# A gated FFT filter and MLP on one core: first MLP product of half the tokens in seven instead of eight block products, tokens outermost; two transform stages on unsplit float32; order made anew

## The chip, the cores and the metric

One core of one Trainium2 chip. The metric is the device time of one execution in microseconds; the runs shown are three executions of the kernel before, and the profile is a further, profiled one.

## The reference

Two branches work on the same x (2048 tokens, 512 features), and a gate per token mixes them. Branch A is a two-dimensional real FFT, a product with learned complex weights, and the inverse FFT. Branch B is an MLP with 1792 hidden units.

```python
def _A_ref(x, w_r, w_i):
    B, S, D = x.shape
    X = (lambda x, axes=(-2,-1): jnp.fft.rfft2(x, axes=axes))(x, axes=(-2, -1))
    W = w_r + 1j * w_i
    X = X * W
    y = (lambda x, s, axes=(-2,-1): jnp.fft.irfft2(x, s=s, axes=axes))(X, (S, D), axes=(-2, -1))
    return y

def _B_ref(x, w1, b1, w2, b2):
    h = jnp.einsum("bsd,df->bsf", x, w1) + b1
    h = _gelu(h)
    return jnp.einsum("bsf,fd->bsd", h, w2) + b2

x = A_x
g = _sigmoid((x * gate_w).sum(-1, keepdims=True))
a = _A_ref(x, A_w_r, A_w_i)
b = _B_ref(x, B_w1, B_b1, B_w2, B_b2)
return g * a + (1 - g) * b
```

## The kernel before

**Split operands.** Everything is float32 outside. For TensorE most operands are split in two tiles of type float32r, a high part h (a copy by ScalarE that rounds) and a low part l (the difference, by VectorE). A product is then three matmuls, h h, h l and l h, added up in PSUM (`prods`, line 506). For most weights the low part is made otherwise (`minus`, line 555): ScalarE writes -h, and an accumulating DMA from GpSimd's queue (`acc`, line 493) adds the weight from HBM.

**MLP** (`mlp`, line 1071). Tokens come in four chunks c of 512; the hidden units in 14 blocks f of 128; features in four blocks q of 128. The first product takes 12 matmuls of 512 columns for each c and f (PSUM tile ph), then gelu in place on ScalarE (line 1127) and the split into g_f h and l (`split`, lines 551 and 552). The second product takes 3 x 7 matmuls for each c and q (PSUM tile po). The hidden blocks go in two halves of seven: all four chunks run with blocks 0 to 6, then all four with 7 to 13. Partial sums go to HBM (bacc). Split x is kept in HBM between the halves (xs, `keep_x`, line 649), and each weight block is loaded and split once (`load_w`, line 1051).

**Transforms.** `forward(j)` (line 686), for 16 groups j of 128 tokens: sums and differences eo and w on VectorE, split of w into eoh and eol (lines 704 and 706), then the feature transform into PSUM tile pd, four matmuls on the high part and four on the low part, whose tables cf hold high and low columns side by side. VectorE splits the result into zb h and l (line 747) and adds the low columns (line 751). Then six matmuls into py, the first token stage. `own_rows` (line 791) mends a few rows with one small product (pown). The later token stages are radix-4 sums on VectorE (`radix4`), and `filt` multiplies by the filter. `inverse(c, h, late)` (line 947) runs eight times with two groups j each: a turn by tables tg (split, lines 956 and 957), its operand pq split into v h and l, eight matmuls into PSUM tile pz, split of pz into zb (lines 990, 991 and 993), and 12 matmuls into pa. Where late is set, its result is added to the output by an accumulating DMA.

**Order.** Each step is entered with its engine, an estimate of its cost, and the buffers that it reads and writes. A planner (`Graph.schedule`, line 311) plays the program through and gives each engine a fixed order. Where several steps are ready, the lowest rank goes first; the ranks are one number a step in the string RANKS. Buffers come in numbered slots per kind, and a step whose buffer has no free slot is passed over. On the chip every engine and queue runs its list in that order. SP issues plain DMAs; GpSimd issues the accumulating ones.

```python
def prods(ps, ah, al, bh, bl, first, last):
    mm(ps, ah, bh, first, False)
    mm(ps, ah, bl, False, False)
    mm(ps, al, bh, False, last)
...
for s, r in zip(g.steps, ranks):
    s.rank = 0.05 * int(r)
order = g.schedule()
```

Of the kernel before, what the change touches and what calls it, by code (L numbers as in the profile page):

```python
# [24 lines left out]
FA = NF // 2  # L25

TE, TW = 320, 576


EXACT = [0, 64, 128, 192]  # L30
NX = len(EXACT)
FORD = np.concatenate([np.arange(1, HD, 2), EXACT, [f for f in range(0, HD, 2) if f not in EXACT], [HD]])
# [23 lines left out]
def _tables():  # L56
# [3 lines left out]
    def cs(c, f):  # L60

        th = 2 * np.pi * np.asarray(f)[None, :] * d / D
        v = -np.sin(th) if c else np.cos(th)
        n = np.array([0.5 if g in (64, 192) else 1.0 for g in f])
        e = np.where(np.abs(v) > 0.6, np.where(n == 0.5, BIG, 1.0), SMALL) * np.sign(v)
        return np.where(np.isin(f, [*EXACT, HD])[None, :], e, v)

    BIG, SMALL = 2276 / 4096, 942.75 / 4096
    factor = np.ones(D)
    factor[128] = np.sqrt(2.0)  # L70
    factor[[64, 192]] = BIG * np.cos(np.pi / 8) + SMALL * np.sin(np.pi / 8)

    cf = np.zeros((2, P, TW), np.float32)
    even = FORD[P + NX:HD]
    for c in range(2):
        h, l = _split(cs(c, FORD[:P]))
        cf[c][:, :P], cf[c][:, P:2 * P] = l, h
        h, l = _split(cs(c, [*EXACT[c:], *even, *([HD] if c else [])]))
        cf[c][:, TE + 2:TE + 2 + P] = h
        cf[c][:, TE + 2 + P:TE + 2 + 2 * P - NX] = l[:, NX - c:P - c]  # L80
        assert not np.delete(l, np.arange(NX - c, P - c), 1).any()
# [8 lines left out]
    ]) / factor[f]  # L90
# [36 lines left out]
    fx = np.stack(_split(fx.reshape(4 * NJ, 4 * NJ)), 1)  # L127
    fx = np.concatenate([fx, fx])
# [306 lines left out]
def tile_kernel(ctx: ExitStack, tc: tile.TileContext, xt, xc, w1, w2, b1, b2, x0g, wf, wrev, out, consts):  # L435
# [41 lines left out]
    def c_pe(n, k=1):  # L477
        return k * (n / 2400 + 0.0135) + 0.005
# [779 lines left out]
    for c in LATE:  # L1258
        stage4(c)
# [63 lines left out]
```

## Time and profile before

| | |
|---|---|
| median of 3 runs | 372.27 us (371.92 to 372.30) |
| span of the profiled execution, first to last instruction | 370.0 us |
| granted TensorE clock, mean | 1.000 |
| DMA moved | 61.20 MB |
| HBM read, written | 41.82 MB, 16.92 MB |

The profile names no other time of its own execution than the span. In rows of groups, `L504` is the helper that records every matmul, so matmuls are told apart by tiles: `ph<-mxh,wa2h` writes PSUM tile ph from operands mxh and wa2h. After the count stand the busy time in us, the mean duration of one in ns, and the idle time of the engine just before it with what ended it. A row of a timeline has the start, the length up to the end of the last one of the row, and how many instructions it merges. In a row of stretches stand from and to, the length, then busy time and count for PE, PEld, DVE, ACT and POOL, the granted clock, the DMA share and GB/s.

### The profile page before, as it was taken

The numbers are of one execution on the slowest core, as the hardware profiler recorded it, in microseconds if no ns is written. First come the engines' busy times: TensorE is split into PE (matmuls) and PEld (weight loads), VectorE is DVE, ScalarE is ACT, GpSimd is POOL, SyncE is SP. The second block draws the span as 40 slices with busy tenths as digits, with TensorE's granted clock in tenths as the row PEclk, the third lists the DMA queues.
The fourth block names the chain that finished last, engine by engine and source line by source line (L and its number), as shares of the span: only waits on it lengthen the run. The fifth ranks groups of instructions, "written<-read, shape, count | busy, mean of one in ns | idle before, by whom it ended". The sixth has DMA issues, their size and how long they took to land.

```text
span 370.0 us, 5589 instructions
## 1 busy us (share of the span) xinstructions
PE 365.0 (99%) x1845; PEld 311.2 (84%) x1845; DVE 337.1 (91%) x748; ACT 224.2 (61%) x415; POOL 34.0 (9%) x54
## 2 busy tenths in 40 slices
PE   8999999999999999999999999999999999999996
PEld 7988888888888888888888888888888888888885
DVE  5999999999999999999989896789688999999993
ACT  5999676678724453555298349753955698653410
POOL 0133000000000000003033010000010000101110
PEclk9999999999999999999999999999999999999999
DMA  8999766195764582586769873216431053276456
GB/s 249 362 267 233 199 201 200 44 271 197 234 222 141 206 288 82 207 217 124 194 161 198 236 167 58 43 37 235 62 51 29 2 204 123 94 177 164 98 155 183
DMA packets 42053, 61.20 MB, mean 165 GB/s; under 512 B 4672, under 2 KB 22528, under 8 KB 41248
## 3 DMA queue, kind: packets, MB, share of 16 engines
q1 hardware_dynamic: 36120, 50.55, 41.5%
q0 software_dynamic: 5472, 9.96, 17.1%
q10 hardware_dynamic: 432, 0.33, 0.3%
q8 instruction: 14, 0.23, 0.2%
q14 instruction: 15, 0.12, 0.2%
HBM read 41.82 MB, written 16.92 MB: 159 GB/s over the span
## 4 chain that ended last, share of the span: by engine, by line
PE 97%; DMA 1%; SPq 1%; ACT 0%; issue 0%; DVE 0%; DVEq 0%
PE ph L504 41%; PE po L504 41%; PE pz L504 4%; PE pd L504 4%; PE py L504 3%; PE pa L504 3%; DMA war<-in_w 1%; PE po_23256r L504 0%; PE po_230r L504 0%; SPq L590 0%; SPq L1060 0%; ACT wa1h L1065 0%; SPq L594 0%; DVE o L1202 0%; PE pown L504 0%
## 5 line engine op out<-in xcount | busy, mean ns | idle before, releaser
L1127 ACT ACTIVATE ph<-ph,b1t 128x512 f32<-128x512 f32 x56 | 36.9, 658 | 51.0 <-PE ph L504 51.0
L963 ACT ACTIVATE sw<-y,al 64x512 f32<-64x512 f32 x32 | 22.9, 721 | 4.6 <-DVE y L826 2.1
L922 DVE TENSOR_TENSOR m<-y,wf 128x514 f32<-128x514 f32 x32 | 20.9, 688 | 0.1
L970 DVE SCALAR_TENSOR_TENSOR pq<-y,al,sw 128x256 f32<-128x256 f32 x32 | 14.6, 480 | 2.9 <-ACT sw L966 2.7
L504 PE MATMUL py<-zb,tf 128*128 128x258 f32 x96 | 16.7, 286 | 0.0
L504 PEld LDWEIGHTS py<-zb,tf 128*128 128x128 f32 x96 | 14.5, 190 | 1.2
L1177 ACT ACTIVATE o<-po,b2t 128x512 f32<-128x512 f32 x8 | 5.4, 688 | 16.6 <-PE po L504 16.5
L778 ACT ACTIVATE y<-pys 64x257 f32<-64x257 f32 x32 | 13.2, 417 | 3.3 <-DVE pys L775 2.6
L495 POOL DMA_DIRECT2D w<-ba x8 | 7.0, 899 | 77.8 <-ACT zb L990 46.2
L504 PEld LDWEIGHTS pa<-zb,ci 128*128 128x128 f32 x96 | 13.1, 190 | 1.0
L504 PE MATMUL pa<-zb,ci 128*128 128x256 f32 x96 | 13.4, 282 | 0.0
L699 DVE TENSOR_TENSOR w<-eo 128x256 f32<-128x256 f32 x32 | 13.0, 418 | 0.1
L696 DVE TENSOR_TENSOR eo<-xf 128x256 f32<-128x256 f32 x32 | 12.9, 416 | 0.0
L704 ACT ACTIVATE eoh<-w 128x512 fp32r<-128x512 f32 (+1 forms) x17 | 10.3, 606 | 4.3 <-DVE w L699 4.3
L495 POOL DMA_DIRECT2D bacc<-o x8 | 7.0, 873 | 63.6 <-ACT o L1181 50.5
L747 DVE TENSOR_TENSOR zb<-pd,zb 128x256 fp32r<-128x256 f32 x32 | 12.5, 417 | 0.3 <-ACT zb L745 0.3
L751 DVE TENSOR_TENSOR zb<-zb,pd 128x256 fp32r<-128x256 f32 (+1 forms) x32 | 12.3, 411 | 0.4
L745 ACT ACTIVATE zb<-pd 128x256 fp32r<-128x256 f32 x32 | 11.1, 384 | 1.6 <-PE pd L504 1.0
L495 POOL DMA_DIRECT2D wa7l<-in_w x1 | 0.9, 872 | 121.3 <-DVE g_1l L552 121.3
L706 DVE TENSOR_TENSOR eol<-w,eoh 128x512 fp32r<-128x512 f32 (+1 forms) x17 | 11.1, 652 | 0.3 <-PE pd L504 0.2
L991 DVE TENSOR_TENSOR zb<-pz,zb 128x512 fp32r<-128x512 f32 x16 | 10.9, 683 | 0.4 <-ACT zb L990 0.3
L990 ACT ACTIVATE zb<-pz 128x512 fp32r<-128x512 f32 x16 | 9.5, 594 | 2.7 <-PE pz L504 2.3
(596 smaller groups left out, 1297.5 us busy)
## 6 DMA issues: line engine op xcount, KB each, us to landing
wf<-in_wf SPq DMA_DIRECT2D x16, 257.0 KB, 3.5
bacc<-o SPq DMA_DIRECT2D x16, 256.0 KB, 2.8
xf<-in_xt SPq DMA_DIRECT2D x14, 256.0 KB, 4.2
wbr<-in_w SPq DMA_DIRECT2D x14, 256.0 KB, 3.6
war<-in_w SPq DMA_DIRECT2D x13, 256.0 KB, 3.9
xm<-in_xc SPq DMA_DIRECT2D x12, 256.0 KB, 4.0
tf<-tf SPq DMA_DIRECT2D x16, 192.0 KB, 3.4
bb<-bacc SPq DMA_DIRECT2D x8, 256.0 KB, 3.7
```

The source lines that it names most:

```text
L495: return add("pool", 2.3 * kb / 340, 3.4, lambda: nc.gpsimd.dma_start(dst(), src(), accum_op=ALU.add), reads, writes, rank)
L504: pe.matmul(ps, w, x, start=start, stop=stop)
L696: v(lambda s=s, op=op: vec.tensor_tensor(eo.ap()[:, s], x.ap()[:, 0:2], x.ap()[:, 2:4], op=op), 256, [x], [(eo, s)], feed)
L699: v(lambda s=s, op=op: vec.tensor_tensor(w.ap()[:, s], eo.ap()[:, :, 0], eo.ap()[:, :, 1], op=op), 256, [eo], [(w, s)], feed)
L706: v(lambda k=k: vec.tensor_tensor(l.ap()[:, k], w.ap()[:, k], h.ap()[:, k], op=ALU.subtract), 256 * len(ps), sub[0] + sub[1], sub[2], feed)
L747: v(lambda c=c: vec.tensor_tensor(segs(xl, c, 0, P + c), segs(ps, c, P, P + 4), segs(xh, c, 0, P + c), op=ALU.subtract), 256, [(ps, c), xh ...
L751: v(lambda o=o, i=i: vec.tensor_tensor(xl.ap()[:, :, o], xl.ap()[:, :, o], ps.ap()[:, :, i], op=ALU.add), 256, [ps], [xl], 0)
L778: a(lambda o=o, i=i: act.activation(Y[j].ap()[o:o + HP, 1], pys.ap()[i:i + HP, 1], AF.Copy), 257, [(pys, 1)], [(Y[j], 1 + k)], 0, more=0.1)
L922: v(lambda mk=mk, k=k, y=y, w=w: vec.tensor_tensor(mk.ap(), y.ap(), w.ap()[:, k:k + 1, :ND].to_broadcast([P, 2, ND]), op=ALU.mult), 514, [ ...
L963: a(lambda sw=sw, y=y, o=o, i=i: act.activation(sw.ap()[o:o + HP], y.ap()[i:i + HP, ::-1, :HD], AF.Copy, scale=al.ap()[i:i + HP, 0:1]), 51 ...
L970: v(lambda sw=sw, pq_=pq_, y=y, j=j, k=k, op=op: vec.scalar_tensor_tensor(pq_.ap()[:, k], y.ap()[:, k, :HD], al.ap()[:, 1 + j:2 + j], sw.a ...
L1127: a(lambda f=f, ps=ps: act.activation(ps.ap(), ps.ap(), AF.Gelu_apprx_tanh, bias=b1t.ap()[:, f:f + 1]), 600, [b1t], [ps], 0.9 if half else ...
```

## The change

Chunks 0 and 1 (CA) keep the first product as it was, but run first, with hidden blocks in three passes (5, 5 and 4). Their x is split from the tiles that the forward transform loads. Chunks 2 and 3 (CB) come behind them, in four passes (4, 2, 4 and 4 blocks). For a unit of two hidden blocks and both chunks, the first product is a product of 2 x 2 blocks with 2 x 2 blocks (two halves of the features inside); it is done with seven block products of six matmuls (`times`). The sums of x blocks (forms 11, t1, t2, 21, t3, 22, t4) are made once, the sums of weight blocks for each unit (`spread_w`). Two PSUM tiles X hold partial results that several outputs share. They are copied by ScalarE into the tiles of other outputs or added by VectorE (`copy`, `plus`), and are taken from the transform's PSUM slots from the first unit on. Since both groups of chunks need the weights, blocks of w2 from the fifth on are written back to HBM once split (ws) and read again; the first four are split again, and w1 is loaded again. Partial sums of a second and later pass are added in HBM by GpSimd's accumulating DMAs (`keep`).

In `forward` and `inverse` the operands of pd and pz stay float32: four matmuls of 129 or 128 columns each, with no split in front and no addition behind. `own_rows` has one float32 matmul. The zb tiles go from four to two of another shape. RANKS is new in full.

```diff
-FA = NF // 2
...
+PASS_A = (range(0, 5), range(5, 10), range(10, 14))
+PASS_B = (range(0, 4), range(4, 6), range(6, 10), range(10, 14))
+CA, CB = (0, 1), (2, 3)
+KEPT = 4
...
-    slots = {"xr": 3, "t2k": 7, "e2": 4, "ttab": 3, "xhl": 4, "w": 29, "hid": 2 * FA,
-             "so": 2, "ba": 2, "bb": 1, "gst": 2, "xm": 2, "pf": 2, "pm": 4, "ti": 1}
-    most = {("pm", "ph"): 2, ("pm", "po"): 2, ("pm", "po0"): 1, ("pm", "py"): 3, ("t2k", "pq"): 2, ("w", "at"): 3, ("w", "bt"): 3}
+    slots = {"xr": 3, "t2k": 7, "e2": 2, "ttab": 3, "xhl": 8, "w": 37, "so": 2, "ba": 2, "pf": 2, "pm": 4, "ti": 1}
+    most = {("pm", "ph"): 2, ("pm", "po"): 2, ("pm", "po0"): 1, ("pm", "py"): 3, ("t2k", "pq"): 2, ("w", "g"): 10, ("w", "gB"): 16,
+            ("w", "ah"): 5, ("w", "al"): 5, ("w", "bh"): 5, ("w", "bl"): 5, ("w", "at"): 2, ("w", "bt"): 2,
+            ("w", "wa"): 13, ("w", "wb"): 8, ("w", "xb"): 4, ("w", "tt"): 2, ("xr", "wr"): 2, ("w", "wt"): 1}
...
+    ws = {(f, k): one(f"sb{f}{k}", [P, D], pool=dp) for f in range(KEPT, NF) for k in "hl"}
...
-        w = buf("t2k", [P, 2, 2, P], F32, f"w{j}", parts=2)
-        h, l = (buf("e2", [P, 2, 2, P], F32R, f"eo{k}{j}", parts=2) for k in "hl")
+        w = buf("e2", [P, 2, 2, P], F32, f"w{j}", parts=2)
...
-        for k in (0, 1) if first else (slice(0, 2),):
-            ps = [k] if first else [0, 1]
-            sub = [[(b, p) for p in ps] for b in (w, h, l)]
-            a(lambda k=k: act.activation(h.ap()[:, k], w.ap()[:, k], AF.Copy), 256 * len(ps), sub[0], sub[1],
-              feed)
-            v(lambda k=k: vec.tensor_tensor(l.ap()[:, k], w.ap()[:, k], h.ap()[:, k], op=ALU.subtract),
-              256 * len(ps), sub[0] + sub[1], sub[2], feed)
...
+        if c in CA:
+            if j < 4:
+                X[c] = new_x(c)
+            split_1(X[c], x, j // 4, c == 0)
...
-        def high(ss=(0, 1), cs=(0, 1)):
-            for s in ss:
-                for c in cs:
-                    o, i = odd if s != c else even
-                    mm(ps.ap()[:, c, o], h.ap()[:, s, c], cft.ap()[:, c, i], s == 0, False)
-        def low():
-            for c in range(2):
-                for s in range(2):
-                    o, i = odd_l if s != c else even_l
-                    mm(ps.ap()[:, c, o], l.ap()[:, s, c], cft.ap()[:, c, i], False, s == 1)
-        if first:
-            for s in range(2):
+        def fold(s, cs):
+            for c in cs:
+                o = slice(HW, 2 * HW) if s == c else slice(0, HW)
+                mm(ps.ap()[:, c, o], w.ap()[:, s, c], cft.ap()[:, c, o], True, True)
+        for s in range(2):
+            if first:
                 for c in range(2):
-                    m(lambda s=s, c=c: high((s,), (c,)), NE, 1, [(h, s), *cf_of(c)], [(ps, c)], 0)
-        else:
-            m(high, NE, 4, [h, cft], [ps], 0)
-        m(low, 236, 4, [l, cft], [ps], 0)
+                    add("pe", c_pe4(HW), 0.25, lambda s=s, c=c: fold(s, (c,)), [(w, s), *cf_of(c)], [(ps, c)], 0)
+            else:
+                add("pe", c_pe4(HW, 2), 0.25, lambda s=s: fold(s, (0, 1)), [(w, s), cft], [ps], 0)
...
-        for o, i in ((slice(0, P), slice(0, P)), (slice(P + NX, 2 * P), slice(3 * P + NX, 4 * P))):
-            v(lambda o=o, i=i: vec.tensor_tensor(xl.ap()[:, :, o], xl.ap()[:, :, o], ps.ap()[:, :, i], op=ALU.add), 256, [ps],
-              [xl], 0)
...
-            vh, vl = split(f"v{j}", "e2", [P, 2, HD], pq_, lambda y: y, 512)
-            ps = buf("pf", [P, 2, 2, 2 * P], F32, f"pz{j}", pool=pq)
-            def some(x, k, high, t=t, ps=ps):
+            ps = buf("pf", [P, 2, 2, P], F32, f"pz{j}", pool=pq)
+            def turn(k, t=t, ps=ps, pq_=pq_):
                 for ft in range(2):
-                    mm(ps.ap()[:, ft, k] if high else ps.ap()[:, ft, k, :P], x.ap()[:, k, ft * P:(ft + 1) * P],
-                       t.ap().rearrange("p a b -> p (a b)") if high else t.ap()[:, 0], high, not high)
-            def rest(some=some, vh=vh, vl=vl):
-                some(vl, 0, False)
-                some(vh, 1, True)
-                some(vl, 1, False)
-            m(lambda some=some, vh=vh: some(vh, 0, True), 256, 2, [t, vh], [ps], FEED)
-            m(rest, 248, 6, [t, vh, vl], [ps], FEED)
-            a(lambda n=n, ps=ps: act.activation(zh.ap()[:, :, :, n], ps.ap()[:, :, :, :P], AF.Copy), 512, [ps], [(zh, n)])
-            v(lambda n=n, ps=ps: vec.tensor_tensor(zl.ap()[:, :, :, n], ps.ap()[:, :, :, :P], zh.ap()[:, :, :, n], op=ALU.subtract),
+                    mm(ps.ap()[:, ft, k], pq_.ap()[:, k, ft * P:(ft + 1) * P], t.ap(), True, True)
+            for k in range(2):
...
+                add("pe", c_pe4(P, 2), 0.25, lambda k=k, turn=turn: turn(k), [t, (pq_, k)], [ps], FEED)
...
-            v(lambda n=n, ps=ps: vec.tensor_tensor(zl.ap()[:, :, :, n], zl.ap()[:, :, :, n], ps.ap()[:, :, :, P:], op=ALU.add),
-              512, [ps], [(zl, n)], FEED)
...
+        if n == "b" and f >= KEPT:
+            for k, b in zip("hl", (h, l)):
+                dma(lambda k=k, b=b: sp.dma_start(ws[f, k].ap(), b.ap().bitcast(F32)), 256, [b], [ws[f, k]])
...
+    def keep(c, q, o, ps, first, sign):
+        where = [(bacc[c], 2 * q), (bacc[c], 2 * q + 1)]
+        def dst():
+            return bacc[c].ap()[:, q].rearrange("p a b -> p (a b)")
+        if first:
+            b = nb2 if sign < 0 else b2t
+            a(lambda: act.activation(o.ap(), ps.ap(), AF.Identity, bias=b.ap()[:, q:q + 1], scale=sign), 600, [b, ps], [o])
+            dma(lambda: sp.dma_start(dst(), o.ap()), 256, [o], where)
+        else:
+            a(lambda: act.activation(o.ap(), ps.ap(), AF.Copy, scale=sign), 512, [ps], [o])
+            acc(dst, lambda: o.ap(), 256, [o], where)
...
+    def early_x():
+        new_forms(("11", "t1", "t2"))
+        for e in range(2):
+            b00, b01, b11 = (raw_x(k, n, e, "xr", "xe") for k, n in ((0, 0), (0, 1), (1, 1)))
+            put("11", e, b00)
+            less(b01, b01, b00)
+            put("t1", e, b01)
+            less(b11, b11, b01)
+            put("t2", e, b11)
+            dma(lambda e=e, b11=b11: sp.dma_start(t2s[e].ap(), b11.ap()), 256, [b11], [t2s[e]])
+    def spread_x():
+        new_forms(("21", "t3", "22", "t4"))
+        for e in range(2):
+            b10, b11, b01 = (raw_x(k, n, e, "w", "xb", [free[CA[0]]]) for k, n in ((1, 0), (1, 1), (0, 1)))
+            t = buf("w", [P, 4 * P], F32, f"tt{e}", cls="tt")
+            dma(lambda t=t, e=e: sp.dma_start(t.ap(), t2s[e].ap()), 256, [free[CA[0]], t2s[e]], [t])
+            put("21", e, b10)
+            less(b01, b11, b01)
+            put("t3", e, b01)
+            put("22", e, b11)
+            less(t, b10, t)
+            put("t4", e, t)
...
+    def spread_w(u, late):
+        f0, f1 = 2 * u, 2 * u + 1
+        H = slice(0, HD), slice(HD, D)
+        r = [buf("xr", [P, D], F32, f"wr{f}", cls="wr") for f in (f0, f1)]
+        for x, f in zip(r, (f0, f1)):
+            dma(lambda x=x, f=f: sp.dma_start(x.ap(), w1[f]), 256, [] if u else t2s, [x])
+        ta = buf("t2k", [P, D], F32, f"ws{u}", cls="ws", parts=2)
+        T = {}
...
+        h, l, b = tile_("0h"), tile_("0l"), tile_("1", 2)
+        a(lambda: act.activation(h.ap(), r[0].ap(), AF.Copy), 512, [r[0], *late], [h])
+        minus(h, l, lambda b: b.ap(), 512, lambda: w1[f0], ([h], [l]), 1)
+        a(lambda: act.activation(b.ap()[:, H[0]], r[1].ap()[:, H[1]], AF.Copy), 256, [r[1], *late], [(b, 0)])
+        v(lambda: vec.tensor_tensor(b.ap()[:, H[1]], r[1].ap()[:, H[1]], b.ap()[:, H[0]], op=ALU.subtract), 256, [r[1], (b, 0)], [(b, 1)])
+        sub(ta, 0, r[1], 0, r[1], 1, ALU.add)
+        sub(ta, 1, ta, 0, r[0], 0)
+        sums("s", ta)
+        sub(r[1], 0, r[0], 0, r[1], 0)
+        sub(r[1], 1, r[0], 1, ta, 1)
+        sums("t", r[1])
...
+            def times(o, i, j, start, A=A):
+                bs, w = A[i]
+                def emit():
+                    k = 0
+                    for e in range(2):
+                        for wi, xi in ((0, 0), (0, 1), (1, 0)):
+                            first = start and k == 0
+                            pe.matmul(o.ap(), w(wi, e), FX[j].ap()[:, xi, e], start=first, stop=k == 5, skip_group_check=not start)
+                            k += 1
+                m(emit, 512, 6, [*bs, FX[j]], [o])
...
+            def done(ps, i, n, u=u):
+                f, c = 2 * u + i, CB[n]
+                gelu(ps, f)
+                if end:
+                    v(lambda: vec.scalar_tensor_tensor(ps.ap(), gb.ap()[:, c], 1.0, ps.ap(), op0=ALU.subtract, op1=ALU.mult),
+                      512, [gb], [ps])
+                G[n, f] = split(f"g{c}_{f}", "w", [P, 512], ps, lambda x: x, 512, cls="gB")
+            times(N[0], "11", "11", True)
+            times(N[1], "s1", "t1", True)
+            copy(X[0], N[0])
+            five = buf("t2k", [P, 512], F32, f"five{u}", cls="five")
+            copy(five, N[1])
+            times(X[0], "s2", "t2", False)
+            times(N[0], "12", "21", False)
+            done(N[0], 0, 0)
+            copy(X[1], X[0])
+            times(X[0], "s3", "t3", False)
+            times(X[1], "s4", "22", False)
+            plus(X[1], X[1], five)
+            done(X[1], 0, 1)
+            plus(N[1], X[0], five)
+            done(N[1], 1, 1)
+            times(X[0], "22", "t4", False)
+            done(X[0], 1, 0)
...
+    early_x()
+    for p in range(len(PASS_A)):
+        for c in CA:
+            mlp(p, c)
     for q0 in range(4):
         filt(q0)
-    for n, c in enumerate(ORDER[:2]):
+    for c in CB:
         stage4(c)
-        inverse(c, 0, False)
-        inverse(c, 1, False)
-    for c in LATE:
+        for h in range(2):
+            inverse(c, h, False)
+    for c in CA[::-1]:
         stage4(c)
-    for c in SECOND:
-        mlp(1, c)
-        if c in LATE:
-            inverse(c, 0, True)
-            inverse(c, 1, True)
+    spread_x()
+    for p in range(len(PASS_B)):
+        fast(p)
+        if p < 2:
+            for h in range(2):
+                inverse(CA[1 - p], h, True)
     ranks = RANKS.split()
     assert len(ranks) == len(g.steps)
```

More of the change, by code (lines that the diff above doesn't have):

```diff
@@ L1152, in mlp @@
[L1152 to L1165 removed]
+            o = buf("so", [P, 4 * P], F32, f"o{p}_{c}{q}", parts=3)
@@ L1196, in last @@
             s = slice(h * 2 * P, (h + 1) * 2 * P)
             y = Y[c + 8 * h + 4 * (q // 2)]
-            if n.start and not b:
+            if end and h:
                 for k, e in enumerate((sp, act)):
```

377 lines of the change are left out of this document (164 added, 213 removed), and 154 rows, old and new, of the table RANKS.

## The prediction

> **What bounds the kernel now.** I read first the page's head, its busy line and its chain of waits, then the busy time by stretch, then the order of time on TensorE.
>
> ```profile
> span 370.0 us, 5589 instructions
> PE 365.0 (99%) x1845; PEld 311.2 (84%) x1845; DVE 337.1 (91%) x748; ACT 224.2 (61%) x415; POOL 34.0 (9%) x54
> PE 97%; DMA 1%; SPq 1%; ACT 0%; issue 0%; DVE 0%; DVEq 0%
> 0.00:12.50 12.50, 10.93 (x67) 10.14 (x67) 8.37 (x27) 7.51 (x15) 0.65 (x16) 1.00 0.88 280
> 12.50:60.80 48.30, 48.30 (x274) 42.25 (x273) 46.33 (x124) 40.43 (x89) 7.19 (x8) 1.00 0.86 240
> 60.80:190.00 129.20, 129.20 (x618) 108.63 (x617) 125.11 (x275) 72.69 (x137) 5.83 (x8) 1.00 0.61 186
> 340.00:370.00 30.00, 26.57 (x143) 22.80 (x141) 22.75 (x49) 6.49 (x11) 3.47 (x4) 1.00 0.57 158
> ```
>
> TensorE has work without a gap from 12.5 us nearly to the end, at full granted clock (1.00 in every stretch). Only 5.0 us are idle, at the start and behind the last matmul. So time is the number of matmuls times their spacing, as long as the other engines keep up. VectorE is the one that might not: it is busy 46.33 of 48.30 and 125.11 of 129.20 us in the middle stretches.
>
> The duration of a matmul holds its drain, so I take spacings, from start to start.
>
> ```profile
> 99.67 0.39 PE L504 MATMUL po<-g_5h,wb5h 128*128 128x512 f32 x1
> ...
> 102.84 0.39 PE L504 MATMUL po<-g_6h,wb6l 128*128 128x512 f32 x1
> 5.49 1.04 PE L504 MATMUL ph<-mxh,wa0h 128*128 128x128 f32 x8
> 6.37 0.33 PE L504 MATMUL ph<-mxl,wa0h 128*128 128x256 f32 x1
> 59.78 0.64 PE L504 MATMUL pd<-cf,eoh 128*128 128x254 f32 x4
> 60.27 0.56 PE L504 MATMUL pd<-cf,eol 128*128 128x130 f32 x4
> 60.67 0.33 PE L504 MATMUL py<-zb,tf 128*128 128x258 f32 x1
> 227.79 0.40 PE L504 MATMUL pz<-tg,v1h 128*128 128x256 f32 x2
> 228.03 0.40 PE L504 MATMUL po<-g_10h,wb10h 128*128 128x512 f32 x1
> 229.41 0.33 PE L504 MATMUL pz<-tg,v1l 128*128 128x128 f32 x2
> 229.58 0.45 PE L504 MATMUL pz<-tg,v1h 128*128 128x256 f32 x2
> 229.87 0.34 PE L504 MATMUL pz<-tg,v1l 128*128 128x128 f32 x2
> 230.04 0.44 PE L504 MATMUL ph<-mxh,wa9h 128*128 128x512 f32 x1
> ```
>
> The first and last of 15 rows give 3.17 / 14 = 0.2264 us for 512 columns; 256 columns take (228.03 - 227.79) / 2 = 0.12. The slope is 0.106 us over 256 columns, 0.416 ns a column, with 0.0136 us fixed. A matmul of 128 columns would be 0.067 by that line, yet eight with a new weight each take (6.37 - 5.49) / 8 = 0.110: there the weight load sets the spacing. The first transform costs 60.67 - 59.78 = 0.89 us per row group j (eight matmuls), the turning stage pz 0.24 + 0.17 + 0.29 + 0.17 = 0.87.
>
> **The change, first on TensorE.** (a) For chunks 2 and 3, seven pairs of hidden blocks need 7 products of 6 matmuls instead of 8: 336 become 294. That is -42 x 0.2264 = -9.5 us. Chunks 0 and 1 and the whole second product keep their counts.
>
> (b) Both unsplit stages become four float32 matmuls of 129 or 128 columns, 128 in all. No float32 matmul stands in this trace. Lowest end: one such matmul costs as much as the 128-column row, 0.110, and the stages come to 16 x (0.44 - 0.89) + 16 x (0.44 - 0.87) = -14.1. Highest end: four partial products, each with its own weight load, 0.44, so 16 x (1.76 - 0.89) + 16 x (1.76 - 0.87) = +28.2. Between them: two operands of two halves make four partial products, which stream 4 x 129 columns, 4 x 129 x 0.416 ns + 0.0136 = 0.228; and two weight loads (a high and a low half, each used twice) make 2 x 0.110 = 0.220. Two reckonings meet, so I take 0.228: 16 x (0.91 - 0.89) + 16 x (0.91 - 0.87) = +1.0 us.
>
> The Trainium skill (FP8 and Floating Point Precision, TensorE Precision Notes) counts four passes for true float32, which at this slope is the 0.228 taken. But the Trainium skill (TensorE: Matmul & The Clock Gate, Weight-path perf modes) says that the fast load is off for float32, with an estimate of columns / 1.2 = 107 ns a load; if each pass had its own, that is 0.43 and +27 us. No float32 load stands in this trace; the row of 0.110 has the plain rate already, which speaks for equal loads.
>
> (c) Small ones: two zero matmuls, +0.45; the own-rows product one float32 matmul of 257 columns (4 x 257 x 0.416 ns + 0.0136 = 0.44) for two of 0.12, +0.2; the last column block split whole, under +0.1. Sum of (a) to (c): -7.8 us.
>
> (d) Handovers. A group's first matmul can come late:
>
> ```profile
> 31.07 0.50 PE L504 MATMUL ph<-mxh,wa6h 128*128 128x512 f32 x1
> 31.40 0.39 PE L504 MATMUL ph<-mxl,wa6h 128*128 128x512 f32 x1
> ```
>
> 0.33 here instead of 0.2264. Seven groups a unit instead of four in the same place are 49 for 28, at up to 0.1 each +2.1; none for those that come in a row. I take +1.0.
>
> Sum: 370.0 - 7.8 + 1.0 = 363.2 us of span. The page gives no time of the profiled execution but this span; the median of the runs is 372.27, 2.3 above it, which I keep: **365.5 us**.
>
> **What must stay beside it.** Prices of the other engines:
>
> ```profile
> L706 DVE TENSOR_TENSOR eol<-w,eoh 128x512 fp32r<-128x512 f32 (+1 forms) x17 | 11.1, 652 | 0.3 <-PE pd L504 0.2
> L751 DVE TENSOR_TENSOR zb<-zb,pd 128x256 fp32r<-128x256 f32 (+1 forms) x32 | 12.3, 411 | 0.4
> L993 DVE TENSOR_TENSOR zb<-zb,pz 128x512 fp32r<-128x512 f32 x16 | 10.9, 682 | 0.2
> L957 DVE TENSOR_TENSOR tg<-ti,tg 128x128 fp32r<-128x128 f32 x16 | 4.6, 285 | 2.0 <-ACT tg L956 2.0
> L552 DVE TENSOR_TENSOR g_2l<-ph,g_2h 128x512 fp32r<-128x512 f32 x4 | 2.7, 684 | 0.2 <-ACT g_2h L551 0.2
> L699 DVE TENSOR_TENSOR w<-eo 128x256 f32<-128x256 f32 x32 | 13.0, 418 | 0.1
> L1127 ACT ACTIVATE ph<-ph,b1t 128x512 f32<-128x512 f32 x56 | 36.9, 658 | 51.0 <-PE ph L504 51.0
> L704 ACT ACTIVATE eoh<-w 128x512 fp32r<-128x512 f32 (+1 forms) x17 | 10.3, 606 | 4.3 <-DVE w L699 4.3
> L956 ACT ACTIVATE tg<-ti 128x128 fp32r<-128x128 f32 x16 | 4.9, 309 | 4.9 <-DVE ti L954 4.7
> L1181 ACT ACTIVATE o<-po 128x512 f32<-128x512 f32 x8 | 4.7, 593 | 7.2 <-PE po L504 7.0
> L495 POOL DMA_DIRECT2D bacc<-o x8 | 7.0, 873 | 63.6 <-ACT o L1181 50.5
> bacc<-o POOLq DMA_DIRECT2D x8, 256.0 KB, 4.1
> xs0l<-mxl SPq DMA_DIRECT2D x4, 256.0 KB, 2.9
> mxh<-xs0h SPq DMA_DIRECT2D x1, 1024.0 KB
> q1 hardware_dynamic: 36120, 50.55, 41.5%
> q0 software_dynamic: 5472, 9.96, 17.1%
> ```
>
> VectorE loses L706, L751, L993, L957 and the 16 low halves of v (0.684 each, 10.9): 49.8 us. It gains 14 of 512 elements for x (eight differences, and 22 low halves instead of 16: 9.6), per unit five of 256 and two of 512 for the weight sums (7 x 3.46 = 24.2) and two additions (14 x 0.684 = 9.6): 43.4. So 337.1 - 6.4 = 331, and 331 / 363 is 91% as before. ScalarE loses 10.3, 4.9 and 16 high halves of v (9.7); it gains some 45 copies at 0.606 (four and a half a unit for the weights, eight for the four w2 blocks split again, six for x; 27.3) and at 0.593 the 21 copies within PSUM products and 24 more evictions (26.7): 224 + 29 = 253 us, 70%. Its order is hidden under TensorE unless a copy stands on the seven-product chain, below.
>
> GpSimd's accumulating DMAs go from 38 to 73 (32 partial sums for 8; 14 + 8 + 4 + 7 weight low halves for 22; 8 outputs as before): 34 + 35 x 0.873 = 65 us of issue, and queue 0 to 33% of the DMA engines. SP's queue drops the x copies (24 of 256 KB out, six of 1024 KB in, 12.6 MB) and adds the w2 copies (20 of 256 KB out and 20 in, 10.5) and 18 reloads of w1 and w2 (4.7), with x some 55 MB for 50.55: 45%. Together 78% instead of 59: room on average. An eviction buffer is held 0.593 + 0.873 + 4.1 = 5.6 us; there are two, so one per 2.8 us. The pass of two hidden blocks fills one per 6 x 0.2264 = 1.36 us, eight in 20.4 us with its unit's products, where 22.4 are needed: 2 us late at most, and the next unit can be done in that time, so 0 to +2 for the range.
>
> **Rivals.** *The seven-product chain stalls TensorE* (slower). All units share one PSUM pair X. Behind a unit's last product X is freed by a gelu (0.658), a copy (0.593) and a low half (0.684), then refilled by a copy (0.593): 2.53 us, against the next unit's two free-standing products, 12 x 0.2264 = 2.72. With empty queues it just holds; if each of these four waits behind one other operation (three on ScalarE, one on VectorE, 2.5 us more), each unit is 2.3 us late. Second products of the pass before can fill it (a pass of four blocks has 96 matmuls, 21.7 us). Where the order places them elsewhere, half the delay stays: 7 x 1.2 = +8, 373.5 us. It decides from 0.97 us a unit (6.8 / 7). For it: ScalarE's work grows most. Against: today TensorE is without a gap from 12.5 to 190 us.
>
> *Float32 loads its weights for each partial product*: 0.44 a matmul, 27 us more, 393 us; three loads, 0.33, 379. This is what the Trainium skill's rule on the fast load would do here if it met every pass. The gain is gone from 0.281 (0.228 + 6.8 / 128). Against it, only that the two reckonings meet.
>
> *VectorE becomes the bound.* 331 us at today's 91% is the span forecast, so nothing is to spare. Splits, which TensorE's first passes wait for, now fall in the half that also has all forward transforms. If 1% of its work is uncounted or idle in the wrong place, 3.6 us: 369.
>
> **How the numbers follow.** Forecast 0.64, with a range of its own from 362.5 to 368.5 (handovers 0 to 2.1, evictions 0 to 2, one more us either way for float32 between 0.220 and 0.236); chain stalls 0.14 at 369 to 379; float32 loads 0.10 at 378 to 393; VectorE 0.12 at 367 to 373. The range for 8 in 10 is 361 to 378: it leaves out most of the float32 case, the worst chain stalls and a float32 cheaper than 0.22. About 0.2%, 0.75 us, is what a measurement of this kernel can tell. Faster: 0.64, a fifth of the chain case (0.03), and over half of VectorE's (0.07), 0.74; within 0.2%, 0.05; slower, 0.21.
>
> **What would show it.** Right: TensorE busy near 357 us and still about 98%; spacing of four float32 matmuls in pd and pz near 0.91; VectorE near 331. Wrong in the float32 step: that spacing at 1.3 or 1.8. Wrong in the chain step: TensorE idle or stretched inside each unit, ended by ScalarE's copy into X or VectorE's low half. Wrong in VectorE's: gaps on TensorE before 200 us, ended by VectorE. If TensorE's busy time falls by 8 and the span does not, the gain went into waits.

## The result and the profile after

The changed kernel takes 384.67 us (median of 4 runs, 383.3 to 387.13) against 372.28 beside it: ratio 1.0342 [1.0304, 1.038]. Measured again with the experiments it took 383.18 us, ratio 1.0277 [1.0246, 1.0308]. The forecast was 365.5, faster; it is slower by 11 to 12 us.

The page of the changed kernel, its span, its busy times and its chain of waits:

```profile
span 383.6 us, 5725 instructions
PE 365.0 (95%) x1808; PEld 301.5 (79%) x1808; DVE 328.8 (86%) x729; ACT 250.9 (65%) x459; POOL 64.5 (17%) x83
...
PE 58%; DMA 11%; issue 10%; ACT 8%; DVE 8%; POOL 2%; SPq 1%; POOLq 0%; DVEq 0%; ACTq 0%
```

The work is what was forecast: VectorE 328.8 us (331 forecast), ScalarE 250.9 (253), GpSimd 64.5 (65). What changed is the chain: TensorE holds 58% of it, not 97%; DMA, ScalarE and VectorE hold 27%. TensorE's busy time is 365.0 as before although 40 matmuls of 512 columns are gone on balance (42 less two of zeros). A matmul is recorded as busy for 0.39 us, while the next one starts after 0.2264 where nothing holds it up, so a wait shorter than the difference hides in busy time. Starts of matmuls tell more. The last row of TensorE in each kernel's order of time, changed kernel first, then the kernel before:

```profile
377.92 0.28 PE L493 MATMUL poB<-g_13h,wb13lb 128*128 128x256 f32 x1
```

```profile
366.29 0.28 PE L504 MATMUL po_23256r<-g_13h,wb13l 128*128 128x256 f32 x1
```

The last matmul starts 11.63 us later with 40 x 0.2264 = 9.1 us less to do: TensorE lost 20.7 us more on its way there than before. Behind it the span has 5.7 us instead of 3.7. 20.7 - 9.1 + 2.0 = 13.6, the difference of the spans.

What TensorE waited for in the changed kernel (us in all, times, longest):

```profile
PE ph L493 <- DVE g_10l L542: 2.3, 1, 2.3
PE ph L493 <- DVE g_8l L542: 1.6, 1, 1.6
PE ux L1159 <- DVE ux L1174: 1.4, 1, 1.4
...
PE ux L1159 <- ACT ux L969: 0.9, 1, 0.9
PE ph1u L1159 <- DVE g_1l L542: 0.8, 1, 0.8
PE ux L1159 <- ACT g_0h L541: 0.8, 1, 0.8
PE ph1u L1159 <- DVE g_3l L542: 0.7, 1, 0.7
```

The two longest stand in the first MLP half, beside the filter; those on `ux` (the pair X) and `ph1u` (a unit's other tile, `N[1]` in the code) stand in the units of seven products. VectorE in turn waited for transfers:

```profile
DVE wf L831 <- DMA wf<-in_wf: 7.5, 5, 3.1
DVE b0d L738 <- DMA y<-ownr: 5.4, 1, 5.4
```

Busy time by stretch (TensorE, its loads, VectorE, ScalarE, GpSimd, then granted clock, DMA share, GB/s), the kernel before and then the changed one:

```profile
100.00:160.00 60.00, 60.00 (x267) 49.64 (x266) 58.37 (x116) 26.23 (x42) 0.87 (x1) 1.00 0.58 193
...
200.00:260.00 60.00, 60.00 (x293) 50.68 (x292) 51.91 (x111) 34.08 (x60) 6.12 (x8) 1.00 0.53 133
```

```profile
100.00:160.00 60.00, 56.06 (x234) 44.37 (x233) 48.65 (x102) 28.09 (x47) 14.02 (x16) 0.97 0.88 203
160.00:200.00 40.00, 40.00 (x178) 33.09 (x178) 38.54 (x78) 23.46 (x43) 10.55 (x12) 1.00 0.88 212
200.00:260.00 60.00, 56.54 (x254) 44.67 (x253) 48.22 (x103) 47.40 (x83) 7.04 (x8) 1.00 0.52 127
```

Two places, then. From 100 to 160 us the DMA engines are busy 0.88 of the time instead of 0.58, VectorE has 9.7 us less work done, TensorE 33 matmuls less. From 200 to 260 us the transfers are as before (0.52), VectorE has room, and TensorE still does 39 matmuls less. A third, smaller loss is the wait of 1.4 us on `ux`, at 346 us. A high DMA share alone costs nothing: from 160 to 200 us it is 0.88 too, and TensorE is busy throughout.

A unit of seven products, in the order of time of the changed kernel (start, duration, engine, and in brackets the idle time before it and its releaser). `ux` is both halves of X:

```profile
205.65 0.70 DVE L1168 TENSOR_TENSOR ph1u<-ux,five 128x512 f32<-128x512 f32 x1
...
206.38 0.66 ACT L969 ACTIVATE ux<-ux,b1t 128x512 f32<-128x512 f32 x1 [1.35 <-DVE ph1u L1168]
...
207.08 0.60 ACT L541 ACTIVATE g_0h<-ux 128x512 fp32r<-128x512 f32 x1
...
207.73 1.66 PE L1159 MATMUL ux<-xft,wa 128*128 128x512 f32 x6 [0.81 <-ACT g_0h L541]
...
209.49 0.69 DVE L542 TENSOR_TENSOR g_0l<-ux,g_0h 128x512 fp32r<-128x512 f32 x1 [1.74 <-PE ux L1159]
...
210.22 0.66 ACT L969 ACTIVATE ux<-ux,b1t 128x512 f32<-128x512 f32 x1 [0.50 <-DVE g_0l L542]
...
211.58 0.74 PE L1159 MATMUL ph1u<-xft,wash 128*128 128x512 f32 x2 [0.82 <-DVE g_1l L542]
```

Read against the code: the GELU at 206.38 is of X's second half, which was ready at 205.62; it waited for VectorE's `N[1] = X[0] + five`, which reads the first half. The product at 207.73 goes into the first half; it waited for the high part of the second half's GELU. The low half at 209.49 reads the second half; it waited for that product. No data passes in any of the three. The waits are in the program itself (each line is an instruction, with what it waits for; +512 is the second half):

```
PE   ux+0   <- x, wa          waits for ScalarE: g_0h <- ux+512
DVE  g_0l   <- ux+512, g_0h   waits for TensorE: ux+0 <- x, wa (the product's last matmul)
ACT  ux+0   <- ux+0, b1       waits for VectorE: g_0l <- ux+512
ACT  ux+512 <- ux+512, b1     waits for VectorE: ph1u <- ux+0, five
```

X is one tensor of two halves of 512 columns, and in these four places the program orders accesses to both halves as one. The hand-made order takes them as separate.

### The profile page after: what moved, and what is told of

Read it like the earlier page. It is cut to its first block, busy times and chain, and to the rows that moved or that the text cites. A ratio compares the mean times of both kernels' runs of the same rounds, so it can differ in the third digit from the quotient of the medians.

```text
span 383.6 us, 5725 instructions
## 1 busy us (share of the span) xinstructions
PE 365.0 (95%) x1808; PEld 301.5 (79%) x1808; DVE 328.8 (86%) x729; ACT 250.9 (65%) x459; POOL 64.5 (17%) x83
## 3 DMA queue, kind: packets, MB, share of 16 engines
q1 hardware_dynamic: 37472, 53.65, 44.2%
q0 software_dynamic: 10512, 19.14, 31.6%
## 4 chain that ended last, share of the span: by engine, by line
PE 58%; DMA 11%; issue 10%; ACT 8%; DVE 8%; POOL 2%; SPq 1%; POOLq 0%; DVEq 0%; ACTq 0%
PE po L493 17%; PE ph L493 14%; PE poB L493 9%; PE ux L1159 6%; PE pd L493 3%; PE py L493 3%; DMA wbr<-in_w 3%; PE ph0u L1159 2%; DMA wb1l<-in_w 2%; PE pz L493 2%; PE ph1u L1159 2%; POOL bacc L484 2%; DMA bacc<-oB 2%; ACT sw L875 2%; DMA y<-ownr 1%
## 5 line engine op out<-in xcount | busy, mean ns | idle before, releaser
L969 ACT ACTIVATE ph<-ph,b1t 128x512 f32<-128x512 f32 x28 | 18.4, 659 | 34.3 <-PE ph L493 32.7
L484 POOL DMA_DIRECT2D bacc<-oB x16 | 13.9, 869 | 70.4 <-ACT oB L1047 56.3
L484 POOL DMA_DIRECT2D bacc<-o x16 | 14.8, 943 | 50.0 <-ACT o L1047 45.9
L493 PEld LDWEIGHTS pz<-tg,pq 128*128 128x128 f32 x128 | 16.4, 191 | 4.5 <-issue 1.2
L1047 ACT ACTIVATE o<-po 128x512 f32<-128x512 f32 x16 | 9.4, 596 | 15.6 <-DMA bacc<-o 11.0
L493 PE MATMUL pz<-tg,pq 128*128 128x128 f32 x128 | 17.5, 278 | 1.4 <-ACT sw L878 0.7
L493 PE MATMUL pd<-cf,w 128*128 128x129 f32 x128 | 17.4, 275 | 0.0
L1159 PE MATMUL ph0u<-xf,wa0h 128*128 128x512 f32 x56 | 17.4, 392 | 0.0
L493 PEld LDWEIGHTS pd<-cf,w 128*128 128x128 f32 x128 | 16.3, 191 | 0.9 <-DVE logit L683 0.3
L1159 PE MATMUL ux<-xft,wa 128*128 128x512 f32 x42 | 11.4, 407 | 3.2 <-DVE ux L1174 1.4
```

The source lines that it names most:

```text
L484: return add("pool", 2.3 * kb / 340, 3.4, lambda: nc.gpsimd.dma_start(dst(), src(), accum_op=ALU.add), reads, writes, rank)
L493: pe.matmul(ps, w, x, start=start, stop=stop)
L969: a(lambda: act.activation(ps.ap(), ps.ap(), AF.Gelu_apprx_tanh, bias=b1t.ap()[:, f:f + 1]), 600, [b1t], [ps]).table = "gelu"
L1047: a(lambda: act.activation(o.ap(), ps.ap(), AF.Copy, scale=sign), 512, [ps], [o])
L1159: pe.matmul(o.ap(), w(wi, e), FX[j].ap()[:, xi, e], start=first, stop=k == 5, skip_group_check=not start)
```

## The experiments

The theories: **A**, the halves of X wait for each other though no data passes. **B**, the chain of sums is too long by itself. **C**, the transfers of the new arrangement come late to VectorE, which works in order. **D**, the unsplit float32 stages are a gain of their own.

**Two tensors for X.** A place of two halves becomes two tensors, everywhere it is used:

```diff
-            self.t = self.pool.tile(self.shape, self.dt, tag=f"{self.tag}_{self.slot}", ...)
+            self.t[k] = self.pool.tile([P, 512], F32, tag=f"{self.tag}_{self.slot}_{k}", ...)
...
-        X = [View(free["X"], k, 1, lambda t, k=k: t[:, k]) for k in range(2)]
+            X[k].ap = lambda k=k: free["X"].bank(k)
```

> The changed kernel with its output and order, but the two halves of the pair X are two tensors of one bank each instead of two halves of one tensor (and the other tiles of that place likewise, with the gate's column sum in two instructions and one addition). In the profile after, TensorE's last product of the first unit into the first half starts at 207.7 us, when ScalarE's upper half of the other half's GELU ends, although it needs nothing of it; four such waits of 0.9 to 1.0 us stand between 207 and 226 us, two of 0.3 by 240 and one of 1.6 at 346. Theory A (the program makes the halves wait for each other): TensorE's waits of 207 to 240 us shrink from 4.4 to under 1 us and the time falls by 4 to 6 us, to 378.5 to 380.5. Theory B (the chain of sums itself is too long for its cover, true dependences only): the same waits stay, ended by VectorE's additions and lows, and the time stays within 1 us of 384.7. Theory C (the loss is in the new order's transfers, in the first half): within 1 us of 384.7 too, and the waits of 107 to 160 us stay under A, B and C alike.

375.37 us, ratio to before 1.0103 [1.0058, 1.0149]: 9.3 us below the first measurement of the change, 7.8 below the second. The edit reaches more than X: the tiles pd, pz and pa have the same place and are parted too. The same moment in its order of time, and the stretch:

```profile
203.50 0.60 ACT L548 ACTIVATE g_0h<-uxk 128x512 fp32r<-128x512 f32 x1
...
204.12 1.52 PE L1172 MATMUL uxk<-xft,wa 128*128 128x512 f32 x6
204.69 0.68 DVE L549 TENSOR_TENSOR g_0l<-uxk,g_0h 128x512 fp32r<-128x512 f32 x1
...
206.92 0.73 PE L1172 MATMUL ph1u<-xft,wash 128*128 128x512 f32 x2
```

```profile
200.00:260.00 60.00, 59.87 (x283) 49.26 (x283) 53.27 (x113) 51.26 (x91) 7.03 (x8) 1.00 0.58 144
```

The product no longer waits, the low half runs beside it, and no wait on X or `ph1u` is left in TensorE's list. TensorE does 283 matmuls in the stretch instead of 254. Counted from the first matmul of the first unit to the last matmul of the kernel, this run is 7.4 us shorter than the first profile of the change and 7.6 shorter than the second. Of these, 4.1 stood in front of matmuls into X and 1.9 in front of those into `ph1u`, the rest mostly in front of pa and pz. So theory A holds, with 6.0 us where it promised 4 to 6; what is left of the 9.3 came from the other parted tiles and from before the units, where the transfers differ from run to run. All sums are still there, so B alone does not hold. The wait of 1.7 us for `g_8l` at 112 us stays, as A, B and C all had it.

**No sums.** The two copies into X, the copy `five` and the two additions of each unit are not issued; the place of every other step is kept.

```diff
-                a(lambda: act.activation(o.ap(), i.ap(), AF.Copy), 512, [i], [o])
+                a(lambda: None, 512, [i], [o])
...
-                v(lambda: vec.tensor_tensor(o.ap(), i.ap(), s.ap(), op=ALU.add), 512, [i, s], [o])
+                v(lambda: None, 512, [i, s], [o])
```

> The changed kernel with the same order, without the five copies and additions of each unit of seven products (partial sums are left out; every product, GELU, split and transfer stays). Theory A (halves wait for each other): the waits between the halves' GELUs, splits and products stay for the most part, so TensorE loses 3 us or more between 200 and 240 us, and the time falls by 1 to 3 us, to 381.5 to 383.5. Theory B (the chain of sums is what stalls TensorE): all of the second half's waits go, 6 us or more, to 378 or less. Theory C (transfers of the first half): within 1.5 us of 384.7.

375.94 us, 1.0134 [1.0084, 1.0185]: the number is B's, not A's 381.5 to 383.5. TensorE's waits on `ux` are gone, but those on the unit's other result remain:

```profile
PE ph1u L1159 <- DVE g_1l L542: 0.8, 1, 0.8
PE ph1u L1159 <- DVE g_3l L542: 0.7, 1, 0.7
```

Taken with the run above: the sums together with the false waits make the chain, and removing either breaks it. With the halves apart the sums fit their cover; that is why the first edit keeps all work and gains as much. The false waits do stay without the sums, as I had thought, but off TensorE's path: in this run's order of time, at 205.27 us, the low half still waits 1.12 us for the product, and at 206.00 the GELU 0.58 for that low half. The product itself no longer comes late, since no addition holds up the GELU in front of it.

**Neither stores nor write-back.** The 20 stores of the split second weight and the two transfers of own rows are not issued; the later loads of that weight read another table of the same size.

```diff
-                dma(lambda k=k, b=b: sp.dma_start(ws[f, k].ap(), b.ap().bitcast(F32)), 256, [b], [ws[f, k]])
+                dma(lambda: None, 256, [b], [ws[f, k]])
...
-            add("sp", 0.2, 2.6, lambda k=k: sp.dma_start(yy.ap()[k * HP:k * HP + 1], ...), [r], Y)
+            add("sp", 0.2, 2.6, lambda k=k: None, [r], Y)
```

> The changed kernel with the same order, without the 20 stores of the split second weight (its later loads read another table of the same size) and without the two transfers that write the corrected own rows back. In the profile after, SyncE's queue sends the filter's rows behind a store that waits for its split, VectorE waits for them, and TensorE stands 2.4 us at 154.9 and then runs nine matmuls at half clock; at 111.5 it stands 1.8 us for a VectorE that waited 5.4 us for the own rows. Theory C (transfers queued in order): these two waits and the slow stretch go, and the time falls by 5 to 7 us, to 378 to 380. Theories A and B: the early time is caught up or lost again later, and the time falls by less than 2 us, to 383 or more.

377.35 us, 1.0141 [1.0126, 1.0156]; C's range was 378 to 380. VectorE's wait for own rows is gone, that for the filter's rows falls from 7.5 us to:

```profile
DVE wf L831 <- DMA wf<-in_wf: 0.8, 2, 0.6
```

TensorE's waits for `g_8l` and `g_10l` are no longer listed, those on X all stay (1.4, 0.9, 0.8, 0.8, 0.7). So C is a second cause, in another place.

**The changed kernel once more, and both edits together.** The run without sums, whose edit touches only the second half, already differed from the change at 155 us, so the change itself was profiled again. (The expectation counts the two-tensor run as untouched up to 195 us as well; but its edit also parts pd, in the first half.)

> The changed kernel itself, unaltered, once more, beside the kernel below: how much of the profile's waits is the same in another execution. If the wait of 2.4 us at 154.9 us belongs to the program, it is there again and the time is 383 to 387. If it is an accident of the transfers (the filter's rows landed 6.9 us after their issue in that profile, 5.1 and 5.8 us in the two runs with other edits that touch nothing before 195 us), it is absent in this profile and the time is 379 to 383.

383.18 us: just inside the first branch by its time, and the second by its profile. The wait at 154 us is down to 0.3 us in TensorE's list, but that at 111 us is longer, and slow matmuls follow it (last section):

```profile
PE ph L493 <- DVE g_8l L542: 1.8, 1, 1.8
```

The waits on X are the same in both profiles to a tenth of a us (0.9, 0.8, 0.8, 1.4). What varies from run to run is which transfer comes late; that one does is in both.

> The changed kernel with the two edits at once: X as two tensors, and neither the stores of the split second weight nor the write-back of the own rows. Each alone came to 375.4 and 377.4. If the two causes stand apart (halves that wait for each other in the second half, transfers in the first), their gains add up but for the wait at 155 us, which both lost: 384.7 - 9.3 - 7.3 + 3 = 371, range 369 to 373. If the second only makes up for the first, the time stays at 375.

370.8 us, 0.9958 [0.9937, 0.9979], as the sum of the two causes had it (371). They stand apart, in the main.

**Each half of that edit alone.**

> The changed kernel with the same order, without the two transfers that write the corrected own rows back into the filter's rows (the stores of the second weight stay). The two edits of the run before last took 7 us together against the first measurement and 6 against the second. If the own rows' way back is the larger part, TensorE's wait at 111 us (1.8 and 2.0 us, the longer one with seven matmuls at half clock behind it) is gone and the time is 379 to 381; if the stores are, that wait is gone too but the time is 381.5 to 383.

> The changed kernel with the same order, without the 20 stores of the split second weight alone (the later loads read another table of the same size). If the stores' traffic is what makes the filter's rows and the corrected rows late, the wait at 154 us is gone, that at 111 us shrinks by half or more, and the time is 378 to 380. If they only fill the wires where nobody waits, the wait at 111 us stays at 1.7 to 2.0 us and the time is 381.5 to 383.

Without the write-back 383.51 us (1.0305 [1.0288, 1.0322]): nothing gained, less than either branch had. The wait at 111 us is gone, and the next one, at 153 us, stands in its place (1.8 us; 2.3 and 0.3 in the two profiles of the change). TensorE's and VectorE's waits of that run:

```profile
PE ph L493 <- DVE g_10l L542: 1.8, 1, 1.8
...
DVE wf L831 <- DMA wf<-in_wf: 7.5, 5, 2.6
```

Without the stores 378.53 us (1.0175 [1.0148, 1.0201]), in the range of the first branch. VectorE's waits:

```profile
DVE b0d L738 <- DMA y<-ownr: 5.1, 1, 5.1
DVE wf L831 <- DMA wf<-in_wf: 3.6, 3, 2.2
```

It still waits 5.1 us for the own rows, but TensorE's wait for `g_8l` is no longer listed; that for `g_10l` is 1.1, where I had it gone. The stores' traffic is the larger part: 4.7 to 6.1 us. Without the own rows' way back as well it was 377.35, 1.2 us less; the intervals of the two runs overlap, so it is not shown that this way back costs anything by itself.

**Another order of the same steps.** X as two tensors, every engine's steps in a sequence of my own making.

> The changed kernel with X as two tensors and another order of the same steps: moved on each engine so that VectorE's lows and the half-weights stand ahead of work that waits for transfers, laid out with the own rows' way back at 4.7 us as the profile shows it and not 2.8. Nothing is left out. If order alone was what remained of the loss, the waits at 112, 284 and 291 us of the two-tensor run shrink and the time is 371 to 374; if the transfers simply take that long for any order of this work, it stays at 375 or more.

377.45 us, 1.0138 [1.0123, 1.0153], 2 us more than the two tensors in the order as given, though the intervals overlap. The waits moved rather than went:

```profile
PE ph L512 <- DVE y L724: 1.7, 1, 1.7
PE po L512 <- DMA wb0l<-in_w: 1.6, 1, 1.6
PE po L512 <- ACT o L1067: 1.5, 1, 1.5
```

This shows that this order is no better, not that none is.

**Float32 stages alone.** The kernel before, with the stages on unsplit float32 (the matmul below for the split ones, no splits of `w`, `v` and `tg`, own rows as in the change). In the first try the priorities were kept and the planner arranged the steps anew; in the second each engine's old sequence was held. The second also has four `zb` tiles and four slots for the float32 operands (`e2`); the first, like the change, has two of each.

```diff
-                    mm(ps.ap()[:, c, o], h.ap()[:, s, c], cft.ap()[:, c, i], s == 0, False)
...
-                    mm(ps.ap()[:, c, o], l.ap()[:, s, c], cft.ap()[:, c, i], False, s == 1)
+                mm(ps.ap()[:, c, o], w.ap()[:, s, c], cft.ap()[:, c, o], True, True)
```

> The kernel before, in its own order and with its own eight products, with only the two transform stages and the own rows on unsplit float32. Theory D (float32 is no loss: 0.80 and 0.83 us for four of its matmuls in the profile after, against 0.89 and 0.87 for the split form): TensorE has 2.2 us less and VectorE some 40 us less, and the time is 369.5 to 371.5, faster than both kernels. Rival (unsplit stages cost TensorE their handovers, one weight load more exposed at each float32 matmul): 373 or more.

> The kernel before with its eight products and, unlike the first try of this, every engine's steps held in the sequence that they had before (a step that is gone is left out of the line, a float32 matmul takes the place of the split one), with only the two transform stages and the own rows on unsplit float32. Nothing is left out. The first try came to 375.3 with TensorE's own work 2.5 us less but its waits 6.4 us more, in the first 100 us. Theory D (float32 is a gain, and the first try's loss was its rearranged order): the waits go back to 4 to 5 us and the time is 369 to 370.5, below both kernels. Rival (the shorter stage no longer covers its handovers, whatever the order): the waits at py's products stay and the time is 372 or more.

The first: 375.29 us, 1.008 [1.006, 1.01], slower than the kernel before by 3. Its waits:

```profile
PE py L485 <- ACT pys L728: 1.0, 1, 1.0
PE py L485 <- issue: 0.8, 1, 0.8
```

The second: 371.8 us, 0.9995 [0.9981, 1.0009], no difference that can be told; its waits are gone, and its busy line reads:

```profile
PE 365.0 (99%) x1845; PEld 309.8 (84%) x1845; DVE 294.3 (80%) x648; ACT 202.8 (55%) x365; POOL 33.9 (9%) x48
```

VectorE has 42.8 us less than before and ScalarE 21.4, TensorE exactly as much, and so is the time. Theory D falls: I had read the gain off the spacing of the float32 rows alone. Here is why, in the changed kernel's order of time (a float32 matmul leaves two records):

```profile
61.95 1.05 PE L493 MATMUL pd<-cf,w 128*128 128x129 f32 x8
62.76 0.97 PE L493 MATMUL py<-zb,tf 128*128 128x258 f32 x6
63.56 0.39 PE L493 MATMUL ph<-mxh,wa4h 128*128 128x512 f32 x1
```

Four float32 matmuls take 0.81 us to the next start, but the six behind them take 0.80 where 6 x 0.12 = 0.72 is due. Together 0.89, what the eight split ones took before. (The split ones left a delay too: the `py` behind them, at 60.67 us of the profile before, took 0.16 to the next start for 0.12. By these rows float32 would be 0.04 us a group cheaper, 1.3 us in 32 groups; the interval of the second try leaves room for 0.7.) The rival's claim, waits whatever the order, falls as well. The first try's 3 us came from its order or from its fewer tiles; the two were not told apart, though its wait on `pys` is for neither `zb` nor `e2`.

## Why the forecast was wrong, step by step

The first two terms hold. (a) -9.5 us: the 42 matmuls are gone. The records have 1274 matmuls of 512 columns for 1317: 42 less, two of zeros more, and three that became six of 256. In the run with both edits the time is below the kernel before, though that run leaves out the stores and the write-back. (b) 0.228 a float32 matmul, +1.0 in all: with the delay it leaves to the next one, 0.89 / 4 = 0.22, and the stage alone changes nothing that can be told. The middle value, on which two reckonings met, was rightly taken, and the rivals on float32 loads fell. In the trace each float32 matmul leaves two records with a weight load each, 0.11 us apart; so the reckoning by two loads can be seen, that by four partial products cannot. The terms for VectorE, ScalarE and GpSimd came out within 1%, and no wait shows VectorE as the bound: it idles 12.9 us on two transfers' waits.

**What failed is (d), the handovers, +1.0 with a bound of 2.1.** The profile shows 20.7 us (and 2.0 more behind the last matmul) where it has 1.0, and (b) and the rest of (c) 1.3. I derived it from a first matmul in a row that came 0.1 us late, as if every producer were done in time. Three things took its place:

| from | to | us |
| --- | --- | --- |
| forecast | 365.5 | |
| both edits together | 370.8 | +5.3 |
| stores and write-back put back | 375.4 | +4.6 |
| X, and the other tiles of its place, as one tensor | 383.2 to 384.7 | +7.8 to 9.3 |

Taken alone from the changed kernel, the second edit gained 5.8 to 7.3.

The last line is the rival I gave 0.14, *the seven-product chain stalls TensorE*, at +8. Its place was right, and its sign of recognition in part: the waits are ended by ScalarE or by VectorE's low half, but by ScalarE's GELU and high half, not by its copy into X, and they do not stand in each unit (two in each of the first two, one at 346 us, ended by VectorE's product with the gate). That its price agrees is partly luck: it was reckoned from other operations standing in front of the chain, at half of 2.3 us in each of seven units, and what the runs show is halves that wait for each other. The reckoning of 2.53 us of chain against 2.72 of cover agrees with the run of two tensors, where no such wait is left. I had seen that "all units share one PSUM pair X", and did not ask whether the program keeps its two halves apart. The kernel before has a case of it: pd is one tensor of two halves there, and its program makes ScalarE's first read of one half wait for the last matmul into the other. TensorE's list of waits shows no cost of it there. A tensor whose parts have separate lives was new with this change, and it could have been weighed.

The second line is the sentence "together 78% instead of 59: room on average". The average was right (44.2 + 31.6%), and the stage tells otherwise: from 100 to 160 us the share went from 0.58 to 0.88, because the stores of the split weight and GpSimd's accumulating DMAs (14.0 us of issue for 0.9) now fall there beside the filter's rows, eight loads for nine before. Without the stores alone it is 0.79; the accumulating DMAs were not taken out by themselves. VectorE runs the filter in order, so a late row holds up the low halves behind it, and TensorE waits for these. This queue behind a waiting instruction was not named in the forecast.

The first line, 5.3 us, is only partly named. In the run with both edits TensorE waits for an eviction buffer (`oB`) and, at 10 us, for a high part of x:

```profile
PE poB L500 <- ACT oB L1058: 1.1, 1, 1.1
...
PE ph L500 <- ACT mxh L641: 1.0, 1, 1.0
```

It also waits 0.6 us each for `pz` and `py`; the span behind the last matmul's start is 1.6 us longer than before (370.3 - 365.0 against 3.7). The evictions were in the range (0 to +2). What the rest is stays open. That a better order would remove it was tried once and not shown.

The range, 361 to 378, missed because each rival was priced alone: chain stalls to 379, late transfers not at all, and no case had both.

## What to carry to other kernels

When steps are rearranged by hand or by a planner around parts of one tensor, look whether the program's own waits know the parts; a pair that is written by one engine and read by two others in turn wants two tensors. Price a handover from the chain behind it, with each engine's queue in order, not from rows in which everything was in time; and take the transfers' share from the stage where they are awaited, not from the mean. A matmul's cost includes what it does to the start of the next one.

## What the runs showed of the hardware

**Half clock after a wait of 2 us.** In the changed kernel's first profile, behind the wait for `g_10l`:

```profile
154.92 0.70 PE L493 MATMUL ph<-mxh,wa12h 128*128 128x512 f32 x1 [2.26 <-DVE g_10l L542]
155.41 0.63 PE L493 MATMUL ph<-mxl,wa12h 128*128 128x512 f32 x1
155.84 0.63 PE L493 MATMUL ph<-mxh,wa12l 128*128 128x512 f32 x1
...
158.40 0.42 PE L493 MATMUL ph<-mxh,wa12l 128*128 128x512 f32 x1
```

Seven spacings of 0.427 us instead of 0.2264: 1.4 us on top of a wait of 2.4 (2.65 from start to start, less the 0.2264 that are due). In the second measurement it came behind the wait at 111 us. The stretch there, and the stretch behind a wait at 153 us in the run without the write-back:

```profile
110.00:116.00 6.00, 5.02 (x15) 4.02 (x16) 6.00 (x11) 0.80 (x2) 0.23 (x1) 0.72 1.01 287
```

```profile
152.00:156.00 4.00, 2.87 (x12) 2.36 (x13) 4.00 (x9) 1.12 (x2) 0.88 (x1) 1.00 1.07 237
```

The two waits differ little: 2.22 us from start to start in the first, 2.16 in the second, and the mean clock of the stretch is 0.72 in one and 1.00 in the other. In the eleven profiles of the change and the experiments, past the first 12 us and up to the last matmul, no wait of 2.16 or less was followed by half clock, and the two longer ones were (2.22 and 2.65).

The length need not be all of it. In the traces' records of the clock it is half from 155.05 to 158.46 us in the first profile and from 111.83 to 115.25 in the second, 3.41 us both times, and the full clock before lasted 150.19 and 105.81 us, 44 and 31 times as long. If it can change only at such steps, as these figures suggest, counting on in steps of 3.41 us puts one inside each of the two waits of 2.16 us (near 111.0 us in the run without sums, near 151.8 in the run without the write-back), while the waits of 2.22 and 2.65 lie between two steps. So does the longest harmless one, of 2.12 us, in the run with another order. Whether 2.16 us between two steps would have been harmless is not shown. The Trainium skill (TensorE: Matmul & The Clock Gate, HAM oscillation) warns of idle gaps above some 3.4 us; here 2.22 us was enough, and the measurement decides.

**Late transfers.** The filter's rows take 4.9 us from issue to landing in the median of the changed kernel, but the load issued at 146 us landed after 6.9 in its profile, and after 5.1 and 5.8 in the two runs that are the same up to there or nearly so. In such a stretch (a DMA share of 0.94 from 145 to 150 us and 1.05 in the next five) a difference of 1 or 2 us in one load is the difference between a short wait on TensorE and 2.4 us plus the slow clock.
